# Top-32 attention and a gated expert layer on one core: value products on alternate halves of the array, VectorE's small work amid the maxima, indirect DMAs kept in order

## The chip, the cores and the metric

One core of a Trainium2 chip runs the whole program. The metric is the device time in microseconds (us) of one execution. The engines named below are TensorE (PE, with its weight loads PEld), VectorE (DVE), ScalarE (ACT), GpSimd (POOL) and SyncE (SP), which issues most DMAs.

## What is computed

For 8 batches of 8 heads, 576 tokens and 64 numbers a head: attention that keeps the 32 largest scores of each query, then a layer that routes the 128 best tokens of each batch through two matrices.

```python
scores = scale * np.matmul(q, k.transpose(0, 1, 3, 2))
kth = np.partition(scores, -top_k, axis=-1)[..., -top_k:-top_k + 1]   # top_k = 32
scores = np.where(scores >= kth, scores, -1000000000.0)
attn = softmax(scores)                                 # the reference writes it out
x = np.matmul(attn, v)            # then (B, H, S, D) -> (B, S, H*D)
scores = np.einsum('bsd,d->bs', x, w_gate)
for b in range(B):
    top_idx = np.argpartition(-scores[b], capacity)[:capacity]        # capacity = 128
    xe = x[b, top_idx]
    ye = np.maximum(xe @ w1, 0.0) @ w2
    g = 1.0 / (1.0 + np.exp(-scores[b, top_idx]))
    out[b, top_idx] = x[b, top_idx] + g[:, None] * ye
```

## The kernel before, in words

**Units.** A unit is a pair of heads for a tile of 128 queries, with all 576 keys. Four tiles of 128 queries give 16 such full units a batch. The last 64 queries (tile `t == J`, with `J` = 4) give 2 units of four heads each: two heads stand in rows 0 to 63 and two in rows 64 to 127. So a batch has 18 units, and the program 144.

**The pipeline.** One loop over `n` (it begins behind `units = [...]`) works on six units at once. In iteration `n` TensorE turns the scores of unit `n - 4` (tile `ptr`, with the cut added from `less`), multiplies queries by keys for unit `n + 1` (`multiply`, tile `ps`), and multiplies the weights of unit `n - 4` by the values (`values`, tile `av`). ScalarE takes exponentials (`pT`, `last`), makes half of the cut (`less`), copies the new scores from PSUM (`sc`), and finds which scores of unit `n - 1` lie above a bound (`sides`). GpSimd makes the other half of the cut of unit `n - 3` (`less`), multiplies scores by sides for unit `n - 1` (two `y<-sc,sides`), and adds eight counting numbers (`y<-steps,seen`). VectorE finds a bound for unit `n` in `find_bound`: 16 maxima over 72 columns each (`cand`), then three rounds of maxima and replacements over the 64 candidates (`best`). It then finds the 32nd score of unit `n - 2` in `find_kth` (`next`, two maxima over 584 columns).

**What sets the order.** The class `InOrder` wraps the engines `pe`, `dve`, `act`, `pool` and `sp`: what is called through it keeps program order on its engine, and its calls all carry line 42 in the profile. What is called as `nc.gpsimd...` is placed by the scheduler. Before the change that holds for the two indirect DMAs of the layer, the gather of `xe` (L590) and the scatter into `out` (L653). ScalarE's work for loads and for the layer is put in the list `late` and taken by `flush()` behind the exponentials.

**The values.** `values` runs, for each of the two heads and each of four groups of 128 keys, one product with 128 queries as weights and 65 columns (64 values and a one, whose product is the sum of the weights). For a unit of tile `J` it runs two products with 64 queries instead, one for each half of the array's columns, in turn. A last product with `vpair` adds the 64 last keys for both heads.

**The small work of VectorE.** When a tile's heads are done, `invert` makes `sums` and `rden` from `xs` at the end of an iteration, `normalise` is GpSimd's multiplication `x<-xs,rden` at the start of the next one, and `gates` is VectorE's dot product `prod<-x,wg` at its end. The layer is the generator `mixture`, one step at each place that `mix_at` names: `gate_row` by DMA; five steps with a rank (`junk`) and a `pick` each; `place_ps`; the gather of `xe`; `xe_ps` and a dot product; three steps `h_ps` (24, 24 and 16 matmuls); four steps `y_ps`; the scatter. All of VectorE's work in it stands at the end of the iteration, behind `next`.

Of the kernel before, what the change touches and what calls it, by code (L numbers as in the profile page):

```python
# [45 lines left out]
def kernel(  # L46
# [123 lines left out]

    late = []

    def flush():
        while late:
            late.pop(0)()


# [129 lines left out]
    def find_bound(sc):  # L307

        w = S // 8
        cand = wkpool.tile([P, 2, 64], FP32, name="cand")
        best = [stats.tile([P, 2, 8], FP32, name=f"best{r}") for r in range(3)]
        for i in range(2):
            for u in range(8):
                dve.max(cand[:, i, 8 * u : 8 * u + 8], sc[:, i, u * w : (u + 1) * w])
        for r in range(3):
            for i in range(2):
                dve.max(best[r][:, i, :], cand[:, i, :])  # L320
            if r < 2:
# [93 lines left out]
    def values(t, g, pT, last, av, vs):  # L415
# [36 lines left out]

    def invert(n, xs, den):
        dve.tensor_scalar_add(out=den[0:n, :], in0=xs[0:n, :, D], scalar1=1e-9)
        rden = stats.tile([P, H], FP32, name="rden")
        dve.reciprocal(out=rden[0:n, :], in_=den[0:n, :])
        return rden

    def normalise(n, xs, x, rden):
# [45 lines left out]
    def mixture(row0, gate, rank, exact=False, over=False):  # L505
# [32 lines left out]
        for t in range(NT):  # L538
            yield
            n = R if t == J else P  # L540
            junk = modpool.tile([P, S], FP32, name="junk", tag="scratch")
            dve.tensor_scalar(
                out=junk[0:n, :],
                in0=gate_row[0:n, :],
                scalar1=gate[0:n, t : t + 1],
                scalar2=None,
                op0=ALU.is_gt,
                op1=ALU.add,
                accum_out=rank[0:n, t : t + 1],
            )  # L550
            if exact:
                break_ties(t, gate, gate_row, rank)
            dve.tensor_scalar(
                out=pick[0:n, t, :],
                in0=slot[0:n, :],
                scalar1=rank[0:n, t : t + 1],
                scalar2=None,
                op0=ALU.is_equal,
            )

        yield
        ps = ps_misc.tile([P, 512], FP32, name="place_ps", tag="misc")
        for t in range(NT):
# [10 lines left out]
        row = modpool.tile([P, 1], FP32, name="row")  # L574
        dve.tensor_reduce(
            out=row, in_=ps[:, 0:2], axis=mybir.AxisListType.X, op=ALU.add
        )
        row_i = modpool.tile([P, 1], I32, name="row_i", bufs=2)
        dve.tensor_scalar(
            out=row_i,  # L580
            in0=row,
            scalar1=row0 if isinstance(row0, float) else row0[:, 0:1],
            scalar2=float(done * S - 1),
            op0=ALU.add,
            op1=ALU.min,
        )
# [22 lines left out]
        g = modpool.tile([P, 1], FP32, name="g")  # L609
        dot(P, xe, g)  # L610
        dve.tensor_scalar_max(out=g, in0=g, scalar1=-88.0)
        late.append(lambda: act.activation(g, g, AF.Exp, scale=-1.0))

        hT = modpool.tile([P, NFC, CAP], FP32, name="hT")
        for f0 in range(0, NFC, 3):
            yield
            if f0 == 3:
                dve.tensor_scalar_add(out=g, in0=g, scalar1=1.0)
                dve.reciprocal(out=g, in_=g)
            fcs = range(f0, min(f0 + 3, NFC))  # L620
# [18 lines left out]
        for fc in range(NFC):  # L639
# [12 lines left out]

        nc.gpsimd.indirect_dma_start(  # L653
            out=out.flatten_outer_dims(),
# [19 lines left out]

    def gates(t, x, gate):
        n = R if t == J else P
        dot(n, x[0:n, t, :], gate[0:n, t : t + 1])
# [16 lines left out]

    load_at = (2, 4, 6, 8, 14, 15, 16, 17, 18)
    first_load_at = range(5, 14)
# [6 lines left out]

    mix_at = (5, 7, 9, 10, 11, 12, 13, 14, 19, 21, 23, 25, 27, 28, 29, 30, 31)
    mix_steps = {}
# [11 lines left out]
    flush()  # L717
    inverting = normalising = None
    of_batch = {}
# [5 lines left out]
    for n in range(-1, N + 6):  # L725
# [6 lines left out]
        if n == 2:  # L732
            load_weights()


        gating = None
        if normalising is not None:
            b, t, xs_, rden = normalising
            rows = R if t == J else P
            normalise(rows, xs_, of_batch[b][0][0:rows, t, :], rden)  # L740
            gating = b, t
            normalising = None

# [51 lines left out]
        if is_unit(n - 4):  # L795
# [6 lines left out]
            keep_values(t4, g4, av, xs)  # L802
        if inverting is not None:
            b, t, xs_ = inverting
            rows = R if t == J else P
            normalising = b, t, xs_, invert(rows, xs_, sums[:, b * NT + t, :])
            inverting = None
        if is_unit(n - 4) and g4 == groups(t4) - 1:
            inverting = b4, t4, xs
        if gating is not None:  # L810
            b, t = gating
            gates(t, *of_batch[b])
            if t == J:
# [6 lines left out]
        if n >= N:  # L820
            for _ in range(2):
                next(mixtures[B - 2], None)
                flush()
        if n in load_steps:
# [8 lines left out]

    flush()
    for b in (B - 2, B - 1):
        for _ in mixtures[b]:
            flush()

# [63 lines left out]
    def general(b, row0):  # L902
# [9 lines left out]
        for t in range(NT):  # L912
# [18 lines left out]
            den = stats.tile([P, H], FP32, name="den")  # L931
            normalise(rows, xs, x[0:rows, t, :], invert(rows, xs, den))
            gates(t, x, gate)
        store(out[bass.ds(b, 1)].rearrange("o s n -> (o s) n"), x)
        rank = stats.tile([P, NT], FP32, name="rank")
        for _ in mixture(row0, gate, rank, exact=True):
            flush()

# [39 lines left out]
```

## Time and profile before

| what | before |
|---|---|
| median of 3 runs | 965.56 us (964.6 to 967.24) |
| the profiled execution | 966.9 us, of which the program's span is 964.8 us |
| busy, share of the span | PE 92%, PEld 74%, DVE 88%, ACT 81%, POOL 76% |
| matmuls | 7791 |
| granted TensorE clock, mean | 0.967 |
| chain that ended last | DVE 40%, PE 37%, POOL 8%, ACT 7%, DMA 4%, issue 3% |

The span is the time from the first instruction to the last. A busy share is an average over the whole span, and here the first 50 us and the last 50 us differ from the middle. The chain follows the last instruction back, at each step to what released it. Matmuls overlap each other, so the distance between the starts of two groups says what a group takes.

### The profile page before, as it was taken

To read this page: it belongs to the slowest core of one execution; us is meant where nothing else is said; L and a number is where in the kernel's file an instruction comes from. 1 tells how busy PE (TensorE), PEld (TensorE's weight loads), DVE (VectorE), ACT (ScalarE), POOL (GpSimd) and SP (SyncE) were. 2 spreads that over 40 slices of the span, in tenths; PEclk is the share of its full clock that TensorE was granted. 3 is DMA by queue.
4 is the path that set the end of the run, shared out by engine and by line. 5 is a ranking of instruction groups with operands and counts; after the bars stand their busy time and mean duration, and the time that the engine had idled before them with its cause. 6 is when DMAs were issued, how large, how long until landed. Compare 5 with 4: busy or idle time off the path is not lost.

```text
span 964.8 us, 24451 instructions
## 1 busy us (share of the span) xinstructions
PE 885.8 (92%) x7791; PEld 718.1 (74%) x7791; DVE 853.4 (88%) x4966; ACT 780.6 (81%) x1883; POOL 736.1 (76%) x800
## 2 busy tenths in 40 slices
PE   5699999889999899999999899998999989998945
PEld 3488778778887778777887778777887778876733
DVE  4879999999999799989999899999999899998140
ACT  3699999879888898889898898888988898887400
POOL 2668999778887988779877888878877888879310
PEclk9599999989999999999999999999999999999968
DMA  5932004111230204121140311412040201000021
GB/s 104 264 85 63 13 2 112 34 45 35 62 85 12 67 13 106 41 50 40 62 85 1 67 23 63 84 34 48 21 119 18 45 2 51 14 12 12 2 71 15
DMA packets 122184, 50.14 MB, mean 52 GB/s; under 512 B 116416, under 2 KB 116416, under 8 KB 121024
## 3 DMA queue, kind: packets, MB, share of 16 engines
q1 hardware_dynamic: 118672, 43.91, 18.8%
q0 software_dynamic: 1792, 4.20, 2.5%
q8 instruction: 64, 1.05, 0.5%
q14 instruction: 72, 0.59, 0.2%
q10 hardware_dynamic: 1584, 0.39, 0.2%
HBM read 36.93 MB, written 11.55 MB: 50 GB/s over the span
## 4 chain that ended last, share of the span: by engine, by line
DVE 40%; PE 37%; POOL 8%; ACT 7%; DMA 4%; issue 3%; SPq 0%; POOLq 0%; ACTq 0%
DVE cand L42 19%; PE av L42 11%; DVE next L42 10%; PE ps L42 8%; PE ptr L42 8%; PE h_ps L42 5%; DVE best L42 5%; POOL y L42 4%; PE y_ps L42 4%; POOL less L42 2%; DVE prod L42 2%; ACT sides L42 2%; DMA row_dram<-gate 2%; ACT sc L42 2%; DVE junk L42 2%
## 5 line engine op out<-in xcount | busy, mean ns | idle before, releaser
L42 POOL TENSOR_TENSOR y<-sc,sides 128x576 f32<-128x576 f32 x288 | 365.5, 1290 | 130.3 <-ACT sides L42 130.0
L42 DVE MAX8 cand<-sc 128x8 f32<-128x72 f32 x2304 | 321.4, 216 | 19.5 <-ACT sc L42 19.5
L42 PEld LDWEIGHTS av<-v,pT 128*128 128x128 f32 (+1 forms) x2560 | 256.7, 182 | 56.9 <-issue 23.5
L42 PE MATMUL av<-v,pT 128*128 128x65 f32 (+1 forms) x2560 | 276.9, 269 | 0.1
L42 POOL TENSOR_SCALAR less<-sc,next 128x576 bf16<-128x576 f32 x144 | 249.8, 1735 | 22.3 <-DVE next L42 16.3
L42 DVE MAX8 next<-y 128x8 f32<-128x584 f32 x288 | 204.8, 752 | 29.3 <-POOL y L42 29.1
L42 ACT ACTIVATE sides<-sc,seen 128x576 bf16<-128x576 f32 x288 | 221.0, 768 | 5.6
L42 PE MATMUL ptr<-ident,sc 128*128 128x128 f32 x1152 | 218.8, 284 | 0.0
L42 PE MATMUL ptr<-out_of_reach,less 128*128 128x128 bf16 x1152 | 209.9, 223 | 0.0
L42 ACT ACTIVATE pT<-ptr 128x512 f32<-128x512 f32 x288 | 167.5, 597 | 39.6 <-PE ptr L42 31.2
L42 PE MATMUL ps<-kT,qT 64*128 64x288 f32 (+1 forms) x1280 | 186.1, 442 | 8.6 <-ACT last L42 4.5
L42 ACT COPY sc<-ps 128x576 f32<-128x576 f32 x288 | 170.0, 649 | 11.3 <-PE ps L42 11.2
L42 PEld LDWEIGHTS ptr<-ident,sc 128*128 128x128 f32 x1152 | 165.4, 144 | 15.1
L42 PEld LDWEIGHTS <-less 128*128 128x128 bf16 x1296 | 135.1, 105 | 34.1 <-POOL less L42 27.0
L42 DVE MAX8 best<-cand 128x8 f32<-128x64 f32 x864 | 148.9, 214 | 0.0
L42 PEld LDWEIGHTS ps<-kT,qT 64*128 64x128 f32 (+1 forms) x1280 | 100.2, 182 | 51.3 <-issue 18.4
L42 ACT ACTIVATE less<-sc,next 128x576 bf16<-128x576 f32 x144 | 112.1, 778 | 17.1 <-DVE next L42 17.1
L42 DVE MATCH_REPLACE8 cand<-best,cand 128x64 f32<-128x64 f32 x576 | 116.0, 209 | 0.0
L42 ACT ACTIVATE last<-ps 128x128 f32<-128x128 f32 x144 | 39.7, 275 | 41.3 <-PE ps L42 40.7
L42 PE MATMUL h_ps<-xeT,w 128*128 128x128 f32 x512 | 64.7, 284 | 3.5 <-ACT xeT L42 1.7
L42 PEld LDWEIGHTS h_ps<-xeT,w 128*128 128x128 f32 x512 | 61.5, 198 | 5.8 <-ACT hT L42 2.4
L42 PE MATMUL av<-vpair,last 128*128 128x130 f32 (+1 forms) x320 | 63.0, 298 | 0.0
(80 smaller groups left out, 843.7 us busy)
## 6 DMA issues: line engine op xcount, KB each, us to landing
rows<-in_k_dram SPq DMA_DIRECT2D x64, 128.0 KB, 3.0
v<-in_v_dram SPq DMA_DIRECT2D x64, 128.0 KB, 3.2
out_dram<-x SPq DMA_DIRECT2D x8, 1024.0 KB, 4.8
rows<-in_q_dram SPq DMA_DIRECT2D x62, 128.0 KB, 2.9
w<-in_moe_w_dram SPq DMA_DIRECT2D x2, 2048.0 KB, 13.1
gate_row<-row_dram SPq DMA_DIRECT2D x7, 288.0 KB, 3.8
last<-in_k_dram SPq DMA_DIRECT2D x8, 128.0 KB, 3.3
vpair<-in_v_dram SPq DMA_DIRECT2D x16, 64.0 KB, 3.5
```

The costliest lines, as they stand in the source:

```text
L42: return lambda *a, **kw: self._tc.keep_in_program_order(fn(*a, **kw))
```

## The change

1. In a full unit `values` runs each product as two, with 64 queries each, on alternate halves of the array's columns (rows 0 to 63 and 64 to 127 of `av`), as the units of tile `J` already do. The product with `vpair` stays whole.
2. VectorE's small work goes into a list `vector_late`, which `flush_vector()` takes between the first 8 and the second 8 of the `cand` maxima of an iteration. That holds for `sums` and `rden`, for the dot products, and for the ranks, picks and row numbers of `mixture`. `normalise` now does `sums`, `rden` and GpSimd's `x` together, and so `x` stands behind `less` and ahead of `y` in GpSimd's queue.
3. The two indirect DMAs are called through `pool`, so they keep program order on GpSimd.
4. Two steps of the load move an iteration earlier. In `mixture` the first rank is put down an iteration earlier (it is taken in the same one as before), and the last two ranks, `place_ps` and the gather come two iterations later.

```diff
     late, vector_late = [], []
+    def flush_vector():
+        while vector_late:
+            vector_late.pop(0)()
+    def flush_both():
+        flush_vector()
+        flush()
...
         for i in range(2):
+            if i == 1:
+                flush_vector()
             for u in range(8):
                 dve.max(cand[:, i, 8 * u : 8 * u + 8], sc[:, i, u * w : (u + 1) * w])
...
             for c in range(J):
-                for h, r in heads:
+                for r in (0, R):
+                    h = heads[-1 if r else 0][0]
                     pe.matmul(
-                        av[r : r + n, i * DE : (i + 1) * DE],
-                        pT[:, i, c, r : r + n],
+                        av[r : r + R, i * DE : (i + 1) * DE],
+                        pT[:, i, c, r : r + R],
                         vt[:, h, c, :],
...
+    def normalise(b, t, xs):
+        n = R if t == J else P
+        den = sums[0:n, b * NT + t, :]
+        divide(n, xs, of_batch[b][0][0:n, t, :], den)
...
+            def choose(t=t, n=n):
...
+            vector_late.append(choose)
...
+        vector_late.append(add_up)
...
-        nc.gpsimd.indirect_dma_start(
+        pool.indirect_dma_start(
             out=xe,
...
+        vector_late.append(score)
...
+                vector_late.append(squash)
...
-        nc.gpsimd.indirect_dma_start(
+        pool.indirect_dma_start(
             out=out.flatten_outer_dims(),
...
-    load_at = (2, 4, 6, 8, 14, 15, 16, 17, 18)
+    load_at = (2, 4, 6, 8, 13, 14, 16, 17, 18)
...
-    mix_at = (5, 7, 9, 10, 11, 12, 13, 14, 19, 21, 23, 25, 27, 28, 29, 30, 31)
+    mix_at = (5, 6, 9, 10, 13, 14, 15, 16, 19, 21, 23, 25, 27, 28, 29, 30, 31)
...
+        gating = normalised
+        if inverting is not None:
+            normalised = inverting[0:2]
+            vector_late.insert(0, lambda a=inverting: normalise(*a))
+            inverting = None
+        else:
+            normalised = None
+        if gating is not None:
+            vector_late.append(lambda a=gating: gates(*a))
...
         if is_unit(n):
             bests[n] = find_bound(scs[n])
+        flush_vector()
         if is_unit(n - 2):
             next8s[n - 2] = find_kth(ys.pop(n - 2))
```

On TensorE, in a full unit in the middle of the program, the values stood before as

```order
L42 MATMUL av<-v_126,pT 128x65 x8
L42 MATMUL av<-vpair_128,last 128x130
L42 MATMUL tr<-ident,rows 128x128 x4
```

and stand in the change as

```order
L42 MATMUL av<-v_126,pT 64x65 x16
L42 MATMUL av<-vpair_128,last 128x130
L42 MATMUL tr<-ident,rows 128x128 x4
```

The other rows of TensorE's queue are the same around it; each of these products becomes two matmuls on the chip.

On GpSimd, around the third scatter (`out_0_dram<-gy`) and the fourth gather (`xe`), the order before was as follows (the numbers are the tiles' own; those of `y`, `less` and `next8` rise from one unit to the next).

```order
L653 DMA out_0_dram<-gy_8702,row_i_6941 4608x512
L42 TENSOR_SCALAR less_8840<-sc_8453,next8_8785 128x576
L42 COPY seen_117<-next8_8785 128x2
L590 DMA xe_8899<-out_0_dram,row_i_8808 128x512
L42 TENSOR_TENSOR y_8790<-sc_8547,sides_8789 128x576 x2
L42 TENSOR_TENSOR y_8790<-steps_122,seen_117 128x2x8
L42 TENSOR_SCALAR less_8944<-sc_8547,next8_8887 128x576
L42 COPY seen_117<-next8_8887 128x2
L42 TENSOR_TENSOR y_8892<-sc_8641,sides_8891 128x576 x2
L42 TENSOR_TENSOR y_8892<-steps_122,seen_117 128x2x8
L42 TENSOR_TENSOR y_8996<-sc_8742,sides_8995 128x576 x2
L42 TENSOR_TENSOR y_8996<-steps_122,seen_117 128x2x8
```

The change has around the same gather, which now comes some units behind the scatter:

```order
L42 TENSOR_SCALAR less_9538<-sc_9112,next8_9483 128x576
L42 COPY seen_117<-next8_9483 128x2
L42 TENSOR_TENSOR y_9601<-sc_9320,sides_9600 128x576 x2
L42 TENSOR_TENSOR y_9601<-steps_122,seen_117 128x2x8
L42 TENSOR_SCALAR less_9650<-sc_9214,next8_9596 128x576
L42 COPY seen_117<-next8_9596 128x2
L42 TENSOR_TENSOR x_8402<-xs_9280,rden_9688 128x512
L42 TENSOR_TENSOR y_9716<-sc_9429,sides_9715 128x576 x2
L42 TENSOR_TENSOR y_9716<-steps_122,seen_117 128x2x8
L42 DMA xe_9724<-out_0_dram,row_i_9615 128x512
L42 TENSOR_SCALAR less_9762<-sc_9320,next8_9711 128x576
```

Before, `y_8790` and `y_8892` stand behind the `less` of the next unit, a whole place late, until two `y` in a row catch up. In the change each `less` is followed by its own unit's `y`, and the gather stands behind a finished `y`.

On VectorE, in an iteration with `sums` and the next one with a dot product, the order before was

```order
L42 MAX next_3088<-y 128x8 x2
L42 TENSOR_SCALAR sums<-xs 128x8
L42 RECIPROCAL rden<-sums 128x8
L42 TENSOR_SCALAR junk,ranks<-gate_row,gate 64x576
L42 TENSOR_SCALAR pick<-slot,ranks 64x128
L42 MAX cand<-sc 128x8 x16
```

and in the change it is

```order
L42 MAX next_3188<-y 128x8 x2
L42 MAX cand<-sc 128x8 x8
L42 TENSOR_SCALAR sums<-xs 128x8
L42 RECIPROCAL rden<-sums 128x8
L42 MAX cand<-sc 128x8 x8
L42 MAX best_3256<-cand 128x8 x2
```

The small instructions moved from behind `next` to between the two halves of the `cand` maxima; the rank and pick that stood with them now come in another iteration.

## Rows read from the trace of the kernel before

**Rows 1.** Busy time in two stretches: us, then each engine's busy us, clock, DMA.
```profile
50.00:120.00 70.00, 68.74 (x627) 57.84 (x628) 65.42 (x406) 67.77 (x167) 58.57 (x65) 1.00 0.23 53
120.00:860.00 740.00, 711.01 (x6452) 582.49 (x6452) 712.34 (x4142) 647.90 (x1569) 611.98 (x653) 0.99 0.20 47
```
**Rows 2.** Waits of the whole run, then of 120 to 860: us, times, longest.
```profile
DVE next L42 <- POOL y L42: 29.1, 22, 4.2
...
DVE next L42 <- POOL y L42: 20.4, 13, 4.2
```
**Rows 3.** Timeline of TensorE, a tile-J unit and a full unit: start, us, what.
```profile
458.01 1.16 PE L42 MATMUL av<-v,pT 128*64 128x65 f32 x32
459.00 0.39 PE L42 MATMUL av<-vpair,last 128*64 128x130 f32 x4
459.32 0.71 PE L42 MATMUL tr<-ident,last 64*128 64x64 f32 x8
...
471.40 2.00 PE L42 MATMUL av<-v,pT 128*128 128x65 f32 x16
473.23 0.44 PE L42 MATMUL av<-vpair,last 128*128 128x130 f32 x2
473.51 0.60 PE L42 MATMUL tr<-ident,rows 128*128 128x128 f32 x4
```
**Rows 4.** Chain that ended last, two units with a step of y_ps.
```profile
521.69 2.21 PE av L42 x18
...
528.32 2.21 PE av L42 x18
```
**Rows 5.** Timeline of VectorE, two iterations without small work between them.
```profile
123.71 2.24 DVE L42 MAX8 cand<-sc 128x8 f32<-128x72 f32 x16
...
128.75 2.24 DVE L42 MAX8 cand<-sc 128x8 f32<-128x72 f32 x16
```
**Rows 6.** Instructions in groups: count, then busy us and mean ns, idle before.
```profile
L42 DVE CUSTOM_DVE_ANT_0 prod<-x,wg 128x512 f32<-128x512 f32 (+1 forms) x40 | 39.4, 984 | 7.6 <-POOL x L42 7.6
...
L42 DVE TENSOR_SCALAR sums<-xs 128x8 f32<-128x8 f32 (+1 forms) x40 | 20.7, 518 | 15.9 <-ACT xs L42 15.9
...
L42 DVE TENSOR_SCALAR pick<-slot,ranks 128x128 bf16<-128x128 bf16 (+1 forms) x40 | 15.0, 374 | 1.4
```
**Rows 7.** Timeline of VectorE's small work and of GpSimd's work beside it.
```profile
69.97 0.34 DVE L42 TENSOR_SCALAR sums<-xs 128x8 f32<-128x8 f32 x1
...
68.57 1.72 POOL L42 TENSOR_SCALAR less<-sc,next 128x576 bf16<-128x576 f32 x1
...
500.58 1.04 DVE L42 TENSOR_SCALAR sums<-xs 128x8 f32<-128x8 f32 x1
...
500.31 1.29 POOL L42 TENSOR_TENSOR y<-sc,sides 128x576 f32<-128x576 f32 x1
...
508.75 0.26 DVE L42 TENSOR_SCALAR pick<-slot,ranks 128x128 bf16<-128x128 bf16 x1
```
**Rows 8.** Timeline around a gather: GpSimd and VectorE.
```profile
533.32 1.99 POOL L42 TENSOR_SCALAR less<-sc,next 128x576 bf16<-128x576 f32 x1 [1.66 <-DVE next L42]
...
535.76 1.05 POOL L590 DMA_INDIRECT xe<-out_dram,row_i  x1 [0.32 <-issue]
...
533.04 0.68 DVE L42 CUSTOM_DVE_ANT_0 prod<-x,wg 128x512 f32<-128x512 f32 x1
...
539.57 1.44 DVE L42 MAX8 next<-y 128x8 f32<-128x584 f32 x2 [1.88 <-POOL y L42]
```
**Rows 9.** Timeline of the end: VectorE and GpSimd.
```profile
916.33 0.16 DVE L42 TENSOR_SCALAR sums<-xs 64x8 f32<-64x8 f32 x1 [13.14 <-ACT xs L42]
...
923.12 0.68 DVE L42 CUSTOM_DVE_ANT_0 prod<-x,wg 64x512 f32<-64x512 f32 x1 [6.40 <-POOL x L42]
...
920.35 1.65 POOL L653 DMA_INDIRECT out_dram<-gy,row_i  x1 [17.90 <-ACT gy L42]
921.48 1.60 POOL L42 TENSOR_TENSOR x<-xs,rden 64x512 f32<-64x512 f32 x1
```

More of the change, by code (lines that the diff above doesn't have):

```diff
@@ L169 @@
     )
-    late = []
+    late, vector_late = [], []
     def flush():
@@ L451, in keep_values, with divide @@
             )
-    def invert(n, xs, den):
-        dve.tensor_scalar_add(out=den[0:n, :], in0=xs[0:n, :, D], scalar1=1e-9)
+    def normalise(b, t, xs):
+        n = R if t == J else P
+        den = sums[0:n, b * NT + t, :]
+        divide(n, xs, of_batch[b][0][0:n, t, :], den)
+    def divide(n, xs, x, den):
+        dve.tensor_scalar_add(out=den, in0=xs[0:n, :, D], scalar1=1e-9)
         rden = stats.tile([P, H], FP32, name="rden")
-        dve.reciprocal(out=rden[0:n, :], in_=den[0:n, :])
-        return rden
-    def normalise(n, xs, x, rden):
+        dve.reciprocal(out=rden[0:n, :], in_=den)
         pool.tensor_tensor(
@@ L540, in mixture @@
             n = R if t == J else P
[L541 to L559, printed above, removed]
+            def choose(t=t, n=n):
+                junk = modpool.tile([P, S], FP32, name="junk", tag="scratch")
+                dve.tensor_scalar(
+                    out=junk[0:n, :],
+                    in0=gate_row[0:n, :],
+                    scalar1=gate[0:n, t : t + 1],
+                    scalar2=None,
+                    op0=ALU.is_gt,
+                    op1=ALU.add,
+                    accum_out=rank[0:n, t : t + 1],
+                )
+                if exact:
+                    break_ties(t, gate, gate_row, rank)
+                dve.tensor_scalar(
+                    out=pick[0:n, t, :],
+                    in0=slot[0:n, :],
+                    scalar1=rank[0:n, t : t + 1],
+                    scalar2=None,
+                    op0=ALU.is_equal,
+                )
+            vector_late.append(choose)
         yield
@@ L574, in mixture, with add_up @@
         row = modpool.tile([P, 1], FP32, name="row")
-        dve.tensor_reduce(
-            out=row, in_=ps[:, 0:2], axis=mybir.AxisListType.X, op=ALU.add
-        )
         row_i = modpool.tile([P, 1], I32, name="row_i", bufs=2)
[L579 to L586, printed above, removed]
+        def add_up(ps=ps):
+            dve.tensor_reduce(
+                out=row, in_=ps[:, 0:2], axis=mybir.AxisListType.X, op=ALU.add
+            )
+            dve.tensor_scalar(
+                out=row_i,
+                in0=row,
+                scalar1=row0 if isinstance(row0, float) else row0[:, 0:1],
+                scalar2=float(done * S - 1),
+                op0=ALU.add,
+                op1=ALU.min,
+            )
+        vector_late.append(add_up)
         yield
         xe = modpool.tile([P, HD], FP32, name="xe", tag="gy")
-        nc.gpsimd.indirect_dma_start(
+        pool.indirect_dma_start(
             out=xe,
@@ L609, in mixture, with score, squash @@
         g = modpool.tile([P, 1], FP32, name="g")
-        dot(P, xe, g)
-        dve.tensor_scalar_max(out=g, in0=g, scalar1=-88.0)
-        late.append(lambda: act.activation(g, g, AF.Exp, scale=-1.0))
+        def score():
+            dot(P, xe, g)
+            dve.tensor_scalar_max(out=g, in0=g, scalar1=-88.0)
+            late.append(lambda: act.activation(g, g, AF.Exp, scale=-1.0))
+        def squash():
+            dve.tensor_scalar_add(out=g, in0=g, scalar1=1.0)
+            dve.reciprocal(out=g, in_=g)
+        vector_late.append(score)
         hT = modpool.tile([P, NFC, CAP], FP32, name="hT")
@@ L617, in mixture @@
             if f0 == 3:
-                dve.tensor_scalar_add(out=g, in0=g, scalar1=1.0)
-                dve.reciprocal(out=g, in_=g)
+                vector_late.append(squash)
             fcs = range(f0, min(f0 + 3, NFC))
@@ L673, in dot, with gates, dot_tile @@
         )
-    def gates(t, x, gate):
+    def gates(b, t):
+        dot_tile(t, *of_batch[b])
+    def dot_tile(t, x, gate):
         n = R if t == J else P
@@ L717 @@
     flush()
-    inverting = normalising = None
+    inverting = normalised = None
     of_batch = {}
@@ L733 @@
             load_weights()
[L736 to L742, printed above, removed]
         if is_unit(n - 4) or is_unit(n + 1):
@@ L802 @@
             keep_values(t4, g4, av, xs)
[L803 to L807, printed above, removed]
         if is_unit(n - 4) and g4 == groups(t4) - 1:
@@ L811 @@
             b, t = gating
-            gates(t, *of_batch[b])
             if t == J:
@@ L822 @@
                 next(mixtures[B - 2], None)
-                flush()
+                flush_both()
         if n in load_steps:
@@ L832 @@
             load_v(v[b + 1], qkv[b + 1][2])
-    flush()
     for b in (B - 2, B - 1):
         for _ in mixtures[b]:
-            flush()
+            flush_both()
     sure = stats.tile([P, 1], FP32, name="sure")
@@ L931, in general @@
             den = stats.tile([P, H], FP32, name="den")
-            normalise(rows, xs, x[0:rows, t, :], invert(rows, xs, den))
-            gates(t, x, gate)
+            divide(rows, xs, x[0:rows, t, :], den[0:rows, :])
+            dot_tile(t, x, gate)
         store(out[bass.ds(b, 1)].rearrange("o s n -> (o s) n"), x)
@@ L936, in general @@
         for _ in mixture(row0, gate, rank, exact=True):
-            flush()
+            flush_both()
     row0 = const.tile([P, 1], FP32, name="row0")
```

## The prediction, made before the change was run

> **What bounds the kernel now.** I read the busy time by stretch first, and not the shares of the whole span, because the start and the end are different work. In the 740 us from 120 to 860 us TensorE is busy for 711.0 us and VectorE for 712.3 us, while ScalarE has 647.9 and GpSimd 612.0 [rows 1]. So two engines are full at once, and each has under 30 us of idle time. The reader should draw two things from it. Freeing one of the two leaves the other, and the most that can be won in this stretch without shortening VectorE's own work is VectorE's idle time, 740.0 - 712.3 = 27.7 us.
>
> Next I read what VectorE waited for. Of those 27.7 us, 20.4 are one wait, for GpSimd's `y` ahead of `next` [rows 2]. The timeline shows where: around the gather, with 1.88 us in one piece [rows 8]. GpSimd sat 1.66 us ahead of a `less`, because that `less` waits for a `next` of VectorE, and the `y` that VectorE wants stands behind it in the queue, with the gather between them as well [rows 8].
>
> Last I looked at what sets the length of a unit. With a step of `y_ps` two units start 528.32 - 521.69 = 6.63 us apart, and the chain runs through TensorE alone there [rows 4]. In iterations without small work VectorE needs 128.75 - 123.71 = 5.04 us [rows 5]. So TensorE sets the units with work of the layer, and VectorE comes a little behind it and catches up elsewhere.
>
> **Values on alternate halves.** The trace of before has this form already, in the units of tile `J`. There 32 matmuls with 64 queries take 459.00 - 458.01 = 0.99 us, against 473.23 - 471.40 = 1.83 us for 16 matmuls with 128 queries [rows 3]. From the first matmul to the next operation it is 1.31 us against 2.11 us [rows 3]. A full unit keeps its whole product with `vpair`, 473.51 - 473.23 = 0.28 us, so it should take 0.99 + 0.28 = 1.27 us, and 0.84 us less than before. Over 128 full units that is 107 us of TensorE. A unit with `y_ps` then takes 6.63 - 0.84 = 5.79 us on TensorE. On VectorE its iteration has 5.04 us and about a rank and a pick, near a microsecond, so VectorE sets it. Over the stretch TensorE falls to about 711 - 107 x 0.84 = 621 us (740 us hold some 107 full units), well under VectorE's 712. What comes off the end is therefore not 107 us, but what VectorE still idles.
>
> The tile-`J` block includes a change to half columns at its start and one back at its end. The Trainium skill says in "TensorEngine Tiling (Array Packing)", Key Properties, that changing the tiling mode drains TensorE, which speaks against doing it in every unit. By that rule a full unit would pay two drains on top; the trace bears it out at most in small part, as 1.31 us holds both changes.
>
> **The indirect DMAs in order.** The list of instructions shows each `y` at its own place again, so the wait of 20.4 us should go nearly whole. What is late next is the gather itself, 1.05 us on GpSimd [rows 8]; it stands behind a finished `y`, and GpSimd is idle for 128 of 740 us. `x` comes between `less` and `y` and holds `y` back by at most its own length, about a microsecond; `y` is wanted only an iteration later. For the stretch I take all but 6.7 of VectorE's 27.7 us: **-21 us**. The rest stays for the ranks that wait for `gate_row`, and for units in which ScalarE or a long `h_ps` is as long as VectorE.
>
> **The small work amid the maxima.** The same instructions run, so in itself this is nothing. Its price is in what they run beside. `sums` takes 0.16 us when GpSimd is idle [rows 9], but 1.04 us when a `y` runs: it began 0.27 us behind the `y` and ended with it, 501.62 against 501.60 us [rows 7]. Beside `less` it also waited, 0.34 us, until that ended at 70.29 us [rows 7]. The dot product took 0.68 us although a `less` began 0.28 us behind it, and that `less` took 1.99 us in place of 1.72 [rows 7, 8]; so `less` does not hold it. `pick` takes 0.26 us where nothing holds it [rows 7], and I take it to be like the dot product. The means are 0.518, 0.984 and 0.374 us [rows 6]. Waiting for GpSimd now costs VectorE 40 x (0.36 + 0.30 + 0.11) = 31 us in all. Where will the work fall? Once VectorE is the bound, ScalarE and GpSimd start `less` as soon as `next` is done, that is at the start of the iteration. The small work begins eight maxima later, about a microsecond, in the midst of `less` (1.72 us). Then the dot products and picks lose most of their waits (16 us at most), and `sums` loses more than now, up to 1.7 us each. I take **-5 us**. The bounds are -31 us, if nothing waits, and +25 us, if half of the 128 small operations (with the 8 dot products on `xe`) wait for a whole `y` of 1.29 us: 64 x 1.29 - 31 = +52, of which I take half, since a VectorE that falls behind lets ScalarE and GpSimd finish `y` earlier relative to it.
>
> A wait in the midst of the maxima holds the second half of `cand`, `best` and `next` behind it. `sums` waits for `xs`, the last work of ScalarE's iteration, where it waited behind `next` before; a VectorE that is the bound has slack there. On ScalarE the exponential of the gate moves behind `pT`, and SP's loads shift by an iteration; both I cost at nothing, under ScalarE's 92 us of idle time in the stretch.
>
> **The start and the end.** From 50 to 120 us VectorE idles 70.0 - 65.4 = 4.6 us [rows 1]; I take **-2 us**. Of the waits for `y`, 29.1 - 20.4 = 8.7 us lie outside the middle [rows 2]; I take **-3 us** behind 860 us, and **-0.8 us** for one unit of values on the last chain. At the very end GpSimd's last `x` stood behind the scatter: `sums` is done at 916.5 us, and `x` begins at 921.48 us [rows 9]. In the change it stands ahead of the scatter. That frees up to 5 us, but the copies of the gates in PSUM, which wait for the same `y_ps`, come next, so I take half, **-2.4 us**, with 0 and -5 as bounds.
>
> The sum is -21 - 5 - 2 - 3 - 0.8 - 2.4 = -34 us. The profiled execution took 966.9 us, 1.3 us over the median of 965.56, so against the median I predict 965.6 - 34 = **932 us**.
>
> **Rivals.** First, *the waits vanish*: the small work meets no `y` at all, and VectorE saves 31 us there instead of 5, which gives 906 us. For it speaks that `less` lies at the start of an iteration; against it that `sums` waits for `less` too. Second, *the drain is paid*: a full unit pays for each change as long as a matmul lasts that is still under way, 0.17 us here (2.00 us of busy time against 1.83 us to the next start [rows 3]). The saving is 0.84 - 2 x 0.17 = 0.5 us, TensorE is at 657 us, VectorE still binds, but the long units cost more of its idle time, say 6 us: 938 us. It is the Trainium skill's rule, from the page named above, as a case of this kernel. Third, *the waits only move*: the small work meets `y` in part, +20 instead of -5, which gives 957 us. Fourth, on the other side, *every small operation meets `y`*: GpSimd runs `y` half of the time and, if ScalarE stays some 1 to 3 us behind VectorE as now, `y` runs just at the eighth maximum. Each of 128 operations then waits half a `y`, 0.64 us or 82 us in all, and each second one, having waited, meets the next `y` as well, another 41. Against the 31 now that is +92 instead of -5, or 1029 us; it decides for slower from about +29 on, when a small operation waits 0.47 us on the mean (0.24 now). Against it stands that such a wait delays VectorE and so draws it out of that phase. Fifth, *the change doesn't do what it says*: the halves do not run side by side, 32 matmuls take 32 x 1.83 / 16 = 3.66 us, TensorE gains 1.83 us a unit, and the time is near 1150 us. The tile-`J` rows speak against it.
>
> **How the numbers follow.** I give the forecast 0.55, the vanishing waits 0.13, the drain 0.12, the waits that only move 0.12, every operation meeting `y` 0.06, and the halves in turn 0.02. Up to 0.3%, 2.9 us, is no difference that a measurement of this kernel can tell, and the three runs differ by as much. The forecast's own range is 918 to 946 us. The range that should hold 8 in 10 takes in the drain, most of the vanishing waits, and the moved waits in part: 908 to 955 us. The first three cases are faster, and so is most of the fourth; of the 0.12 of moved waits I give 0.04 to no change and 0.01 to slower, and of the last two all 0.08 to slower, less 0.01 for an end near the old time. Faster 0.87, the same 0.05, slower 0.08.
>
> **What would show it.** In the profile of the changed kernel the group `av<-v,pT` should have 4608 matmuls of 64 queries, and a full unit's values should take near 1.27 us. In 120 to 860 us VectorE should be busy over 97% and TensorE under 90%, and `next` should wait for `y` under 5 us in all. `sums` should be longer in the mean than 0.52 us, the dot product and `pick` shorter than 0.98 and 0.37 us. If VectorE's idle time grows, or the waits of the small work exceed 50 us, I am wrong on the time; if values take over 1.8 us a unit, on the mechanism.

## The result, and the profile after

The changed kernel takes 922.17 us (median of 4 runs, 919.48 to 924.62) beside 966.4 us for the kernel before, measured together. The ratio is 0.9537, with a 95% interval of 0.9496 to 0.9578. In a later series the same kernel took 929.65 us (6 runs, 927.62 to 933.04) beside 966.35: 0.962 [0.958, 0.966]. Faster was right, and both times lie in the range. The gain of 44 us (37 in the second series) stands beside 34 forecast, but of the three terms behind it only the first had the right size: VectorE's idle time, VectorE's small work, and the start and end gave -18.8, -20.7 and -3.8 us in the profiled executions, where -21, -5 and -8.2 were forecast.

The page of the changed kernel, engines and chain:

```profile
PE 808.6 (88%) x9839; PEld 617.3 (67%) x9839; DVE 832.5 (90%) x4966; ACT 772.5 (84%) x1883; POOL 732.4 (79%) x800
...
DVE 35%; PE 28%; ACT 20%; POOL 6%; DMA 5%; issue 4%; SPq 0%; POOLq 0%; ACTq 0%
```

To compare the same work, the span is cut at two score products `ps<-kT,qT`: that of unit 19, the second of the second batch, and that of unit 140, with the units counted from 0 (the expectations name the second cut by its iteration, 139). The timelines of TensorE have them at 120.22 and 859.68 us before, and at 116.09 and 816.07 us after. The busy times of the stretches between and behind them are, before and after:

```profile
120.22:859.68 739.46, 710.47 (x6448) 582.12 (x6446) 711.80 (x4141) 647.45 (x1568) 611.43 (x652) 0.99 0.20 47
859.68:964.80 105.12, 74.46 (x577) 56.80 (x575) 44.93 (x227) 40.52 (x98) 42.81 (x43) 0.87 0.11 25
```
```profile
116.09:816.07 699.98, 646.09 (x8160) 499.02 (x8159) 691.09 (x4148) 640.93 (x1568) 606.83 (x651) 0.99 0.22 50
816.07:921.50 105.43, 70.67 (x689) 51.92 (x687) 45.64 (x232) 40.25 (x98) 42.57 (x44) 0.85 0.11 26
```

So the start gave 4.1 us, the middle 39.5, and the end lost 0.3. In the middle VectorE is busy for 98.7% now, TensorE for 92.3%. VectorE idles 8.9 us where it idled 27.7, and is busy 20.7 us less.

VectorE's waits in the whole run [rows 2]; the wait for `y` lies outside the middle altogether, and of the middle's idle time 5.9 us wait for `gate_row`:

```profile
DVE next L42 <- POOL y L42: 6.2, 6, 2.9
...
DVE junk L42 <- DMA gate_row<-row_dram: 5.9, 7, 1.5
```

The small work in groups [rows 6], and two `sums` beside a `less` and one beside a `y`, from the timelines of VectorE and GpSimd [rows 7]:

```profile
L42 DVE CUSTOM_DVE_ANT_0 prod<-x,wg 128x512 f32<-128x512 f32 (+1 forms) x40 | 30.6, 765 | 2.4 <-POOL x L42 2.4
L42 DVE TENSOR_SCALAR pick<-slot,ranks 128x128 bf16<-128x128 bf16 (+1 forms) x40 | 15.5, 387 | 1.4
L42 DVE TENSOR_SCALAR sums<-xs 128x8 f32<-128x8 f32 (+1 forms) x40 | 12.4, 310 | 17.5 <-ACT xs L42 17.5
```
```profile
476.00 0.15 DVE L42 TENSOR_SCALAR sums<-xs 128x8 f32<-128x8 f32 x1
...
475.21 1.72 POOL L42 TENSOR_SCALAR less<-sc,next 128x576 bf16<-128x576 f32 x1 [0.18 <-POOL y L42]
...
556.72 0.66 DVE L42 TENSOR_SCALAR sums<-xs 64x8 f32<-64x8 f32 x1
...
556.61 1.73 POOL L42 TENSOR_SCALAR less<-sc,next 128x576 bf16<-128x576 f32 x1
...
543.97 1.14 DVE L42 TENSOR_SCALAR sums<-xs 128x8 f32<-128x8 f32 x1
...
543.80 1.28 POOL L42 TENSOR_TENSOR y<-sc,sides 128x576 f32<-128x576 f32 x1
```

The first `sums` begins 0.79 us into a `less` and runs at full speed. The second begins 0.11 us into one and is held until 0.77 us into it. The third ends where its `y` ends (545.11 against 545.08 us). The timelines of the whole run have 25 `sums` that lie within a `less` and beside nothing else of GpSimd's. The 18 that begin 0.60 to 0.80 us in take 0.14 to 0.17 us. The five that begin 0.11 to 0.49 us in take 0.27 to 0.66 us, and all end 0.76 or 0.77 us in. Two begin 0.04 us in and take 0.17 us. On the timeline of TensorE, two neighbouring units with a step of `y_ps` [rows 3, 4]:

```profile
480.06 1.15 PE L42 MATMUL av<-v,pT 128*64 128x65 f32 x32
...
485.98 1.15 PE L42 MATMUL av<-v,pT 128*64 128x65 f32 x32
487.06 0.49 PE L42 MATMUL av<-vpair,last 128*128 128x130 f32 x2
487.39 1.88 PE L42 MATMUL y_ps<-w,hT 128*128 128x512 f32 x4
```

The products take 1.08 us, the whole block 1.41, and the units stand 5.92 us apart. Both engines are full there: in the view by stretches, three such units from 480.06 us on take 17.77 us, of which TensorE is busy for all and VectorE for 17.70.

The end, from the timelines of GpSimd, VectorE and TensorE [rows 9], first the drain of the pipeline, then the last tile:

```profile
823.08 1.66 POOL L42 DMA_INDIRECT out_dram<-gy,row_i  x1 [0.16 <-issue]
824.24 2.28 POOL L42 TENSOR_SCALAR less<-sc,next 128x576 bf16<-128x576 f32 x1
...
826.58 0.23 PE L42 MATMUL ps<-out_of_reach,less 128*128 128x128 bf16 x1 [2.32 <-POOL less L42]
...
873.11 0.16 DVE L42 TENSOR_SCALAR sums<-xs 64x8 f32<-64x8 f32 x1 [13.16 <-ACT xs L42]
...
878.78 0.81 DVE L42 TENSOR_SCALAR_CACHE_REDUCE junk<-gate_row,gate 128x576 f32<-128x576 f32 x1 [3.37 <-ACT gate_row L42]
...
873.65 1.03 POOL L42 TENSOR_TENSOR x<-xs,rden 64x512 f32<-64x512 f32 x1 [14.43 <-DVE rden L42]
```

And the chain that ended last, behind that tile, before and after:

```profile
930.55 3.35 DMA xe<-out_dram,row_i
```
```profile
877.13 4.92 DMA out_dram<-gy,row_i
882.62 3.95 DMA out_dram<-x
887.38 3.40 DMA xe<-out_dram,row_i
```

### The profile page after: what moved, and what is told of

Read it like the earlier page. It is cut to its first block, busy times and chain, and to the rows that moved or that the text cites. A ratio compares the mean times of both kernels' runs of the same rounds, so it can differ in the third digit from the quotient of the medians.

```text
span 921.5 us, 28585 instructions
## 1 busy us (share of the span) xinstructions
PE 808.6 (88%) x9839; PEld 617.3 (67%) x9839; DVE 832.5 (90%) x4966; ACT 772.5 (84%) x1883; POOL 732.4 (79%) x800
## 4 chain that ended last, share of the span: by engine, by line
DVE 35%; PE 28%; ACT 20%; POOL 6%; DMA 5%; issue 4%; SPq 0%; POOLq 0%; ACTq 0%
DVE cand L42 18%; DVE next L42 8%; ACT sides L42 7%; PE ptr L42 7%; PE ps L42 6%; ACT sc L42 5%; PE av L42 5%; PE h_ps L42 5%; DVE best L42 5%; PE y_ps L42 5%; ACT pT L42 3%; POOL y L42 2%; POOL less L42 2%; DMA row_dram<-gate 2%; DVE prod L42 2%
## 5 line engine op out<-in xcount | busy, mean ns | idle before, releaser
L42 DVE MAX8 cand<-sc 128x8 f32<-128x72 f32 x2304 | 331.5, 217 | 16.0 <-ACT sc L42 16.0
L42 POOL TENSOR_SCALAR less<-sc,next 128x576 bf16<-128x576 f32 x144 | 256.7, 1783 | 26.9 <-DVE next L42 17.9
L42 ACT ACTIVATE pT<-ptr 128x512 f32<-128x512 f32 x288 | 163.2, 597 | 32.3 <-PE ptr L42 26.7
L42 PEld LDWEIGHTS av<-v,pT 128*64 128x64 f32 x4608 | 147.2, 138 | 57.5 <-ACT pT L42 30.7
L42 PE MATMUL av<-v,pT 128*64 128x65 f32 x4608 | 167.5, 225 | 0.3 <-ACT pT L42 0.2
L42 ACT ACTIVATE less<-sc,next 128x576 bf16<-128x576 f32 x144 | 113.2, 786 | 10.2 <-DVE next L42 9.8
L42 PE MATMUL ps<-out_of_reach,less 128*128 128x128 bf16 x144 | 32.2, 224 | 42.0 <-POOL less L42 42.0
L42 PE MATMUL av<-vpair,last 128*128 128x130 f32 (+1 forms) x320 | 69.0, 316 | 0.0
```

The lines of the kernel that those rows point to most:

```text
L42: return lambda *a, **kw: self._tc.keep_in_program_order(fn(*a, **kw))
```

## The experiments

Three parts can be made apart: halves (H), small work amid the maxima with the shifted steps (A), indirect DMAs in order (O). "Wait for y" is `next<-y` of the whole run, with the part in the middle in brackets. "Middle" and "end" are cut at units 19 and 140 as above, in the profiled run. Times are medians; the kernel before took 965.95, 969.32, 966.35 and 966.14 us beside runs e1 to e4, e5 to e7, the next four, and e11.

| run | parts | us | ratio to before [95%] | wait for y (in the middle) | middle | VectorE busy there | end |
|---|---|---|---|---|---|---|---|
| before | none | 966.4 | | 29.1 (20.4) | 739.5 | 711.8 | 105.1 |
| e1_halves | H | 957.09 | 0.9911 [0.988, 0.9943] | 24.8 (17.2) | 734.2 | 708.8 | 107.3 |
| e2_order | O | 951.76 | 0.9859 [0.9836, 0.9882] | 20.2 (11.3) | 727.2 | 706.2 | 106.0 |
| e3_amid | A | 946.57 | 0.9794 [0.976, 0.9827] | 8.4 (1.5) | 725.1 | 707.5 | 102.8 |
| e4_amid_order | A, O | 951.8 | 0.9879 [0.985, 0.9907] | 8.4 (0) | 727.7 | 714.4 | 106.6 |
| e5_halves_amid | H, A | 927.37 | 0.956 [0.953, 0.959] | 7.8 (1.8) | 707.8 | 690.1 | 102.9 |
| e6_halves_order | H, O | 944.98 | 0.9746 [0.9719, 0.9774] | 6.2 (0) | 724.1 | 709.8 | 104.1 |
| changed | H, A, O | 922.17 | 0.9537 [0.9496, 0.9578] | 6.2 (0) | 700.0 | 691.1 | 105.4 |
| changed_again | H, A, O | 929.65 | 0.962 [0.958, 0.966] | 4.8 (0) | 706.4 | 693.2 | 105.1 |
| e7_halves_apart | H by turns undone, A, O | 941.07 (1 run) | | 6.2 (0) | 717.5 | 698.9 | 104.4 |
| e8_rank_later | H, A, O | 923.02 | 0.9541 [0.9502, 0.9579] | 5.3 (0) | 699.0 | 696.0 | 105.5 |
| e9_rank_later_free | H, A | 915.65 | 0.9476 [0.9436, 0.9517] | 7.6 (1.5) | 695.9 | 691.3 | 102.2 |
| e10_scatter_later | H, A, O | 920.7 | 0.9529 [0.9489, 0.9569] | 6.2 (0) | 696.8 | 693.8 | 107.5 |
| e11_shift | shifted steps alone | 975.14 | 1.009 [1.006, 1.012] | 36.5 (27.5) | 752.2 | 713.5 | 104.6 |

**e1_halves**: the kernel before with the halves alone.

```diff
-                for h, r in heads:
+                for r in (0, R):
+                    h = heads[-1 if r else 0][0]
...
-                        av[r : r + n, i * DE : (i + 1) * DE],
-                        pT[:, i, c, r : r + n],
+                        av[r : r + R, i * DE : (i + 1) * DE],
+                        pT[:, i, c, r : r + R],
```

> The kernel before with only the value products of full units on alternate halves. Theory A (VectorE's accounts: the time of the middle is VectorE's busy time plus its idle time, and TensorE's relief counts only as far as VectorE idled for it): the wait of next for y around the gathers stays, about 20 us, and so do the waits of the small work for GpSimd; only the few us that VectorE idled for TensorE go, so 956 to 965 us. Theory B (TensorE's own time is what was paid): 107 us less TensorE shows as 30 us or more, below 935 us.

Theory A held, with 957.09 us: TensorE's busy time in the middle fell from 710.5 to 655.0 us, and only 5.3 us of that came off, since VectorE stayed at 708.8.

**e2_order**: the kernel before with `pool.indirect_dma_start` in place of `nc.gpsimd.indirect_dma_start`, twice, and nothing else.

> The kernel before with only the two indirect DMAs kept in order. Theory A: VectorE's 20 us of waiting for y go, but TensorE, busy for 711 of 740 us, binds at once, so about half comes through: 950 to 960 us. Theory B: the DMAs' place is nothing while TensorE binds: within 3 us of 966.

Theory A held for the time, 951.76 us. But the wait for `y`, which the order was to remove, is still the longest of VectorE's in the middle, with 11.3 of the whole run's 20.2 us there, while TensorE is busy for 704.7 of the middle's 727.2 us:

```profile
DVE next L42 <- POOL y L42: 20.2, 31, 3.1
```

**e3_amid**: the changed kernel without halves and with the scheduler's indirect DMAs.

> The kernel before with only the small work amid the maxima (and the steps that move for it); values whole, DMAs placed by the scheduler. Theory A: VectorE's waits for GpSimd fall by up to 20 us, but TensorE's 711 us stand against it and the wait for y stays: 955 to 966 us. Theory B (the small work's place is worth its 20 us alone): 946 us or less.

Theory A missed, and theory B is missed by 0.6 us only: 946.57 us. In the middle the wait for `y` went without any order (1.5 us stay), and was partly exchanged for one for `gate_row`:

```profile
DVE junk L42 <- DMA gate_row<-row_dram: 11.3, 7, 3.6
DVE next L42 <- POOL y L42: 8.4, 13, 2.5
```

**e4_amid_order**: the changed kernel with whole value products.

> The changed kernel with whole value products as before. Theory A: TensorE binds in the units with work of the layer, its 711 us in the middle leave at most 29 us: 940 to 955 us, and TensorE is busy for over 96% of the middle. Theory B (TensorE's relief was not needed): within 5 us of 922.

Theory A held, 951.8 us, with TensorE busy for 703.1 of 727.7 us. But VectorE is busy for 714.4 us there, so it is as full as TensorE; `pick` alone takes twice as long in the mean as in the changed kernel (785 against 387 ns):

```profile
L42 DVE TENSOR_SCALAR pick<-slot,ranks 128x128 bf16<-128x128 bf16 (+1 forms) x40 | 31.4, 785 | 1.4
```

With the small work amid the maxima, the order gains nothing in the middle (725.1 and 727.7 us) and loses 3.8 at the end. The halves are worth 30 us on top of these two parts (22 by the changed kernel's second series), and 9 alone. The units with `y_ps` stand 6.63 us apart as before, by the timeline of TensorE:

```profile
491.10 2.00 PE L42 MATMUL av<-v,pT 128*128 128x65 f32 x16
...
497.73 2.00 PE L42 MATMUL av<-v,pT 128*128 128x65 f32 x16
```

**e5_halves_amid**: the changed kernel with `nc.gpsimd.indirect_dma_start`, twice.

> The changed kernel with its indirect DMAs back on the scheduler's choice (halves and small work amid the maxima kept). Theory A: with the steps shifted the scheduler's own place for the DMAs is no longer bad (in the run with the small work alone VectorE's find_kth waited 8.4 us for GpSimd's y, against 29.1 us before the change), so the order adds nothing to the other two parts: 917 to 928 us, find_kth waiting under 12 us for y, and the stretch after the last unit of position 139 2 to 4 us shorter than with the order (105.4 us). Theory B: the order is what lets VectorE fill up once the halves have freed TensorE: without it some 15 to 20 us of waits for y stay, 935 us or more.

Theory A held, 927.37 us, with a wait for `y` of 7.8 us and an end 2.5 us shorter. The middle is 7.8 us longer than the changed kernel's, and 7.0 of that are `junk`'s; beside the changed kernel's second series (706.4 us) it is 1.4 us longer. By the ratios, 0.956 beside 0.9537 and 0.962, the order adds nothing to the other two parts that can be told:

```profile
DVE junk L42 <- DMA gate_row<-row_dram: 12.9, 7, 3.7
DVE next L42 <- POOL y L42: 7.8, 13, 2.5
```

**e6_halves_order**: the kernel before with the edits of e1 and e2.

> The kernel before with halves and in-order indirect DMAs, the small work left behind find_kth and the steps not shifted. Alone, the halves gave 9 us (957.1) and the order 14 us (951.8); together as a plain sum 943. Theory A: each of the two still leaves a wait of VectorE on GpSimd (find_kth for y was 24.8 us with the halves alone, 20.2 with the order alone), so VectorE keeps some 20 us of idle time: 935 to 943 us. Theory B: once the order has made room in GpSimd, the halves are enough and the small work's place doesn't matter: 920 to 928 us, find_kth waiting under 10 us.

The median lies 2 us above theory A's range, 944.98 us, and for another reason than either theory gave. The wait for `y` is gone from the middle, where the halves alone left 17.2 us, yet VectorE is as busy as before (709.8 us), since the small work behind `next` meets `y` and is held by it:

```profile
DVE next L42 <- POOL y L42: 6.2, 7, 2.6
```
```profile
L42 DVE CUSTOM_DVE_ANT_0 prod<-x,wg 128x512 f32<-128x512 f32 (+1 forms) x40 | 43.3, 1083 | 7.6 <-POOL x L42 7.6
```

From here to the changed kernel are 23 us (15 by its second series), and VectorE's busy time in the middle falls by 709.8 - 691.1 = 18.7 us. That is what the place amid the maxima gives, together with the shifted steps; `junk`'s wait for `gate_row` has another 5.2 us (11.1 to 5.9).

**e7_halves_apart**: the changed kernel with the halves one behind the other.

```diff
-            for c in range(J):
-                for r in (0, R):
+            for r in (0, R):
+                for c in range(J):
```

> The changed kernel with the same 64-query products, but all 16 chunks' products of the left half issued before those of the right half, instead of by turns. Theory A: what saves TensorE's time is that two products on different halves of the array's columns run beside each other, which they do only by turns: a full unit's values then take 1.8 us or more (as whole products, 1.83), the units whose score products follow stand 6.6 us or more apart again instead of 5.93, and the time is 945 to 965 us. Theory B: the time of a product goes by its 64 columns whatever the order: values stay at 1.1 to 1.3 us, and the time at 922 us.

Neither size came out. The products take 486.04 - 484.56 = 1.48 us on TensorE's timeline, against 1.08 by turns and 1.83 whole:

```profile
484.56 1.55 PE L42 MATMUL av<-v,pT 128*64 128x65 f32 x32
486.04 0.49 PE L42 MATMUL av<-vpair,last 128*128 128x130 f32 x2
```

Turns are worth 0.40 us a full unit: units with `y_ps` stand 6.32 us apart here (489.60 and 495.92 us), against 5.92. The span, of a single run, is 18 us longer (939.2 against 921.5; 13.5 against the second series' 925.7), but `junk`'s wait for `gate_row` grew by half as much, from 5.9 to 14.7 us. The other 0.35 us come with the smaller products themselves; why 32 products of 64 queries are shorter than 16 of 128 even in a row, these runs don't tell.

**changed_again**, with the next three on the same chip:

> The changed kernel once more, beside the next three on the same chip: 920 to 925 us, as before (922.2).

Missed, 929.65 us. Of the middle's 6.4 us more, VectorE's busy time has 2.1, and the wait that grew is `junk`'s, from 5.9 to 9.8 us:

```profile
DVE junk L42 <- DMA gate_row<-row_dram: 9.8, 7, 2.3
```

**e8_rank_later**: `mix_at = (5, 7, 9, ...` in place of `(5, 6, 9, ...`.

> The changed kernel with the first of the three rank steps at iteration 7 instead of 6 (its compare, junk, waits 5.9 us in all, seven times, for the DMA that brings gate_row). Theory A: VectorE sets the pace of the middle, so what it does not wait is gained: 4 to 6 us less than the changed kernel in the same call, 916 to 919 us. Theory B: the wait is only put elsewhere (xe or y come late instead): no difference over 2 us.

The difference came as theory A has it, a little larger: 923.02 against 929.65 us, though the time itself is above its range, as the changed kernel's was. The wait for `gate_row` is gone from the list, the middle is 699.0 against 706.4 us. So the changed kernel's time hangs on when that DMA lands. Beside the changed kernel's first series, 922.17 us, nothing is gained.

**e9_rank_later_free**: e8 with the scheduler's indirect DMAs.

> As e8_rank_later, but with the indirect DMAs on the scheduler's choice. Without the order, e5_halves_amid lost 7.8 us in the middle against the changed kernel and gained 2.5 at the end; junk's wait for gate_row was 12.9 us there, 7.0 more. Theory A: that wait is nearly all of what the order is worth on top of the other two parts, so with the step at iteration 7 the order is worth nothing and the shorter end decides: 914 to 918 us, at most e8_rank_later. Theory B: the order is worth 6 to 8 us by itself: 920 to 926 us.

Theory A held: 915.65 us, 7.4 less than e8. This is the fastest version, and beats both kernels. Of the 8.1 us between the profiled spans the middle has 3.1, the end 3.4 and the start 1.6. With the indirect DMAs in order `less` is longer in the mean (1793 ns in e8, 1737 in e9), and TensorE waits longer for it; its waits in e8, then in e9:

```profile
PE ps L42 <- POOL less L42: 38.6, 34, 3.6
```
```profile
PE ps L42 <- POOL less L42: 24.1, 40, 1.5
```

**e10_scatter_later**: e8 with the scatter put in a list that is taken behind GpSimd's copy of `seen`.

```diff
-        pool.indirect_dma_start(
+        pool_late.append(
+            lambda: pool.indirect_dma_start(
...
             pool.tensor_copy(out=seen[:, 1, at : at + 2], in_=kth[:, :, 7])
+        flush_pool()
```

> As e8_rank_later, with the scatter kept in order but issued behind the next unit's copy of seen and before its y, instead of before its less. In the changed kernel less takes 2.28 us behind the scatter instead of 1.72, and TensorE waits 2.3 us for it in the drain. Theory A: TensorE loses less in the drain and the stretch after position 139 becomes 1 to 3 us shorter than 105.4 us; in the middle VectorE is full and nothing is gained: 1 to 3 us less than e8_rank_later. Theory B: y comes late in its place and find_kth waits for it: same time or 1 to 3 us more.

The time is 2.3 us less (920.7), as theory A has it, but the runs of e8 and e10 overlap (920.39 to 925.11 and 919.64 to 924.88), so a gain is not shown. Theory A's reason is ruled out: the end got longer, 107.5 us. TensorE's wait for `less` behind the scatter went (2.33 us in e8), and a longer one came, for `pick`, in the timelines of e8 and of e10:

```profile
825.61 0.23 PE L42 MATMUL ps<-out_of_reach,less 128*128 128x128 bf16 x1 [2.33 <-POOL less L42]
```
```profile
828.68 0.18 PE L42 MATMUL place_ps<-place,pick 64*128 64x2 bf16 x1 [4.69 <-DVE pick L42]
```

**e11_shift**: the kernel before with the tables of steps alone.

```diff
-    load_at = (2, 4, 6, 8, 14, 15, 16, 17, 18)
+    load_at = (2, 4, 6, 8, 13, 14, 16, 17, 18)
...
-    mix_at = (5, 7, 9, 10, 11, 12, 13, 14, 19, 21, 23, 25, 27, 28, 29, 30, 31)
+    mix_at = (5, 7, 9, 10, 13, 14, 15, 16, 19, 21, 23, 25, 27, 28, 29, 30, 31)
```

> The kernel before with the tables of steps alone shifted (place, gather and xe two iterations later, two of the load steps one earlier; the rank steps stay), small work still behind find_kth, whole value products, indirect DMAs on the scheduler's choice. e3_amid had this shift together with the small work amid the maxima: 946.6 us, find_kth waiting 8.4 us for y against 29.1. Theory A: it is the later gather that takes the wait for y away: 948 to 956 us, wait for y under 15 us, and sums, prod and pick stay long (518, 984 and 374 ns). Theory B: it is the small work's place that does it: 961 us or more, wait for y over 20 us.

Theory B held, 975.14 us: without the small work amid the maxima the later steps only cost. The wait for `y` is longer than in any other run:

```profile
DVE next L42 <- POOL y L42: 36.5, 37, 2.5
```

## Why the prediction was right, and where it was not

**The frame held.** VectorE now sets the middle, at 98.7%. TensorE was relieved by less than forecast: it is busy for 646.1 us, 92.3%, where the text had 621 us and said under 90%. The block of values is 1.41 us and not 1.27, so a unit with `y_ps` takes 5.92 us and not 5.79, and there both engines are full. Over some 107 units the 0.14 us are an estimated 15 of the 25 us that TensorE is above the forecast; the rest was not followed. The 0.14 us are also what is left for the rival of the drain, which priced it at 0.34. From a score product to the first value product TensorE's timelines have 1.17 us before and after (120.22 to 121.39 and 816.07 to 817.24 us), so going into the halves shows no time of its own. The Trainium skill says in "TensorEngine Tiling (Array Packing)", Key Properties, that a change of the tiling mode drains TensorE, and also that different tiles load weights and multiply in parallel. The second sentence agrees with e7, where turns save 0.40 us; for the first the 0.14 us are the most that these rows leave.

**VectorE's idle time: the size was right, but the order earned little of it.** The forecast was -21 us and the middle shows -18.8 (27.7 to 8.9); of what stays, 5.9 us are the ranks' wait for `gate_row`, as the text had it. The step is "The list of instructions shows each `y` at its own place again, so the wait of 20.4 us should go nearly whole". With the halves it holds: the order takes the wait in the middle from 17.2 us (e1) to nothing (e6). With the order alone 11.3 us stay (e2), where TensorE is busy for 97% of the middle. But the order was not needed. With the small work amid the maxima 1.5 us stay without order or halves (e3), and 1.8 with the halves (e5), so in the changed kernel either part is enough. That this is the place of the small work and not the shifted steps is read from e11, where the steps alone let the wait grow to 27.5 us; the place without the shift was not run, so it is not shown that the place alone is enough. The order of VectorE's instructions gives a reason that fits, though no run isolates it: the small work now runs ahead of `next`, while GpSimd finishes the `y` that `next` wants, and no longer behind it. In e8 and e9 the order costs 7.4 us. So the size was right while the part that it was put down to earned little, which is luck.

**The small work: -5 us forecast, -20.7 us of busy time in the middle.** It was placed rightly, in the midst of `less`, but the step "`sums` loses more than now, up to 1.7 us each" was wrong. It took a `sums` that begins 1.41 us into a `less` and is held until its end [rows 7] to mean that a `less` holds a `sums` wherever it begins. After the change most begin 0.8 us in, and these take 0.15 us; those that begin 0.1 to 0.5 us in are held, but only until 0.77 us in. The mean went to 0.310 us where over 0.52 was said; the dot product fell from 0.984 to 0.765 us, as said; `pick` did not get shorter (0.387 us, said below 0.37). By the groups this is 8.3 and 8.8 us less in the whole run, and 0.5 us more [rows 6]; the other 4 us lie in other groups and were not followed. The first rival, in which the waits vanish, was nearer on this term. The Trainium skill says in "SBUF — State Buffer", Who interferes with whom, that a VectorE instruction with two SBUF inputs, or in a two-port mode, and a GpSimd instruction that reads SBUF exclude each other, whoever starts first. The rows agree for `y`; for `less`, which reads SBUF as well, they agree for its beginning and its end and not for its middle.

**Only together.** H, O and A alone gave 9, 14 and 19 us; the sum, 42, is near the 44 of all three by chance. H and A without the order gave 42 us (969.32 - 927.37) where their sum alone is 28, so these two make the gain. O on top of A loses 5 us (946.57 and 951.8, measured together), and H on top of A and O gains 30, or 22 by the second series. That two engines were full at once, and that H frees TensorE and A frees VectorE, explains part of it: in e1 VectorE stays full (708.8 us busy), in e3 and e4 TensorE does (706.4 and 703.1 us). But A alone takes only 4.3 us off VectorE's busy time (711.8 to 707.5), and the halves on top take 23.3 us off it (714.4 in e4 to 691.1), most of that in `pick`: without the halves six of e4's 40 `pick` last 2.3 to 3.6 us beside GpSimd's `y`, and none does in the changed kernel. Why the small work meets `y` more often when TensorE is full, no run shows.

**Start and end.** The start gave 4.1 us and not 2. The end was to give 6.2 and lost 0.3. The drain was to be 3.8 us shorter and is 0.4 longer: from the cut at unit 140 to the last `sums` 873.11 - 816.07 = 57.0 us, before 916.33 - 859.68 = 56.7 [rows 9]; a `less` behind the scatter takes 2.28 us, and TensorE waits 2.32 us for it. The last `x` stands ahead of the scatter as said, and the ranks begin 2.5 us sooner: from the last `sums` to the first `junk` 5.7 us, before 8.1 (its first `junk` began at 924.48 us). But that won nothing. The chain now leads from the scatter through the last store into `out` to the gather, 877.13, 882.62 and 887.38 us, and the gather begins 10.2 us behind the scatter, as it did before (920.35 and 930.55 us). The step that failed is "I take half, -2.4 us": it followed the ranks and their copies and had no term for that store. No run was made on this piece.

**The rivals.** Waits that only move (957 us), every small operation meeting `y` (1029) and halves in turn (1150) did not come. The last is e7's arrangement in part, and costs far less than it said (941.07 us), since products of 64 queries are shorter even in a row.

## What to carry to other kernels

Where two engines are full at once, try the parts of a change in pairs: alone each looks like little (9 us for the halves), and one that seems to remove a wait may be paying for nothing (the order) once another has removed it. Where a small operation is held by a neighbour engine, list several rows by how far into the neighbour's operation it begins; here that decided between 0.15 us and four times as much. And a transfer that just arrives in time is worth an iteration of margin: moving one step of a table gave 6.6 us beside the slower of two series of the same kernel (nothing beside the faster), and took away the wait that differed between them.

## What the runs showed of the hardware

- VectorE's `sums` (0.15 us alone) is held by GpSimd's `y` (two inputs) until its end: 1.14 us in the row shown. A `less` (one input, 1.72 us) holds it at its beginning and at its end, but not in between: begun 0.11 us in it took 0.66 us, begun 0.60 to 0.80 us in 0.14 to 0.17 us, begun 1.41 us in 0.34 us.
- In a full unit 32 value products of 64 queries take 1.08 us on alternate halves of the columns and 1.48 us half by half; 16 of 128 queries take 1.83 us. Going into and out of the halves cost at most 0.14 us a unit.
- A `less` that starts 1.2 us after the start of a scatter took 2.27 to 2.29 us in all six cases of the changed kernel's middle and drain, alone 1.72; in e10 a pair of `y` there took 3.07 us, elsewhere 2.5. Behind a gather a `y` took its usual 1.29 us before the change.
